# A two-layer decode attention step, forward and backward: score matmuls in column groups, one row layout for both layers, and a fixed TensorE order

## The chip, the cores and the metric

The kernel runs on one core of a Trainium2 chip. The metric is the device time of one execution in microseconds (us). Short names: TensorE is PE in the profile, VectorE is DVE, ScalarE is ACT, and SP (SPq for its queue) is the engine whose queue issues nearly all the loads.

## The reference

Two identical layers, each attention over a cache and then an MLP, and the gradients with respect to all inputs. One new token for each of 2 batches, 32 query heads on 4 key-value heads, 16384 cached keys, head size 128; all in bf16.

```python
x = x + attn(layernorm(x), k_cache, v_cache, wq, wo)   # layer 0
x = x + mlp(layernorm(x), w1, b1, w2, b2)              # layer 1
x = x + attn(layernorm(x), k_cache, v_cache, wq, wo)   # the same weights and cache again
x = x + mlp(layernorm(x), w1, b1, w2, b2)
out, vjp = jax.vjp(f, x, k_cache, v_cache, wq, wo, w1, b1, w2, b2)
return out, *vjp(grad_out)
```

The K and V caches are 33.5 MB each, and dK and dV have the same size. The attention that comes first in the network is called layer 1 here and the second one layer 3.

## The kernel before

The kernel goes over K and V four times: the two forward passes, the backward pass of layer 3 (dq alone, with P kept from the forward), and a last pass that does the backward of layer 1 and writes dK and dV for both layers. The first three are called "the three passes". Each has 8 chunks of 8.39 MB, and a chunk is four groups of 512 keys. K and V of a chunk come as 16 tiles of 512 KB (one for each of the 8 pairs of batch and kv head) into a ring of 24 buffers.

```python
def load_units(src4d, c, tag):                    # 8 loads of 512 KB
    units = []
    for g in range(NG):                           # NG = 8
        b, hk = divmod(g, HKV)
        u = AP_["ring"].tile([128, R, 128], BF, name="u_" + tag, tag="u")
        nc.sync.dma_start(u[:], src4d[b, hk, c * CH:(c + 1) * CH, :].rearrange("(p r) d -> p r d", r=R))
        units.append(u)
    return units

def xpose_group(units, r0, pool, tagname):        # 32 transposes, 4 evacuations (1 on ScalarE, 3 on VectorE)
    ...

def acc_matmuls(acc_ps, XT, units, l, r_list, r_off, first, last):   # O = P V, and dq = dS K
    for i, r in enumerate(r_list):
        for g in range(NG):
            j = 2 * l + g // 4                    # two of the four column groups for each layer
            nc.tensor.matmul(acc_ps[32 * j:32 * j + 32, (g % 4) * 128:(g % 4 + 1) * 128],
                             lhsT=XT[:, i, 32 * (g // 4):32 * (g // 4) + 32],
                             rhs=units[g][:, r_off + r, :], ..., tile_position=(0, 32 * j))

def attn_fwd_pass(l):
    rows = slice(64 * l, 64 * l + 64)             # each layer has its own 64 rows of P
    def XK(gi): ...                               # loads of a chunk, transposes of K
    def S(gi):                                    # scores, maximum, exponential
        sp = ps("mm").tile([128, 512], F32, name="sp", tag="mm")
        for g in range(NG):
            nc.tensor.matmul(sp[:], lhsT=qT_pad[l][:, g, :], rhs=d["kT"][:, g], start=(g == 0), stop=(g == NG - 1))
        ...                                       # reduce_max, min, Exp into P_sb, l_run
    def PT(gi): ...                               # 4 transposes of P, 1 evacuation
    def PV(gi): ...                               # O_g = acc_matmuls(...), O_sb = O_sb * beta + O_g
    XK(0); S(0)
    for gi in range(G):                           # G = 32 groups
        if gi + 1 < G: XK(gi + 1)
        if gi >= 1: PV(gi - 1)
        PT(gi)
        if gi + 1 < G: S(gi + 1)
    PV(G - 1)

def attn_bwd3_pass():                             # the same shape: XV, DP, DST, DQ
    ...
```

The order of calls in this loop is the order in which the program is written. A scheduler then decides the order on each engine, and in the kernel before it is free to do so on TensorE too. `qT_pad[l]` holds for each g a 128-column stationary matrix of which 8 columns are not zero, so that all 8 matmuls can add into one bank.

Of the kernel before, what the change touches and what calls it, by code (L numbers as in the profile page):

```python
# [36 lines left out]
def kernel(  # L37
# [35 lines left out]
    popen("wpool", 4)  # L73
    popen("wtp", 4)
    WP = dict(key="wpool", tag="w", shape=[128, WS])
# [202 lines left out]
    def proj_bwd(W, Din, Dout, dybf, name, cache=None):  # L278
# [9 lines left out]

        def gen():
            for view, j0, nj, n0, ncols in w_slabs(W, Din, Dout):  # L290
                for i in range(nj):
                    nblk = ncols // 128
                    for kb in range(0, nblk, 8):
                        yield (view, i, j0 + i, n0 // 128 + kb, kb, min(8, nblk - kb))

        def T(it):
            view, i, j, jn0, kb, nb = it
            tp = ps("tr").tile([128, 8, 128], BF, name="tp_w", tag="tr")
            for k in range(nb):
                nc.tensor.transpose(tp[:, k, :], view[:, i, (kb + k) * 128:(kb + k + 1) * 128], ident_bf[:])  # L300
            wT = P("wtp").tile([128, 8, 128], BF, name="wT", tag="wT")
            evac(wT[:, 0:nb], tp[:, 0:nb], "bf")
            return wT
# [106 lines left out]
    def build_pad(dst_pad, src_ps, l, mul=None):  # L410
        for g in range(NG):
            b, hk = divmod(g, HKV)
            o = dst_pad[:, g, 64 * l + 8 * g:64 * l + 8 * g + 8]
            i = src_ps[:, 8 * hk:8 * hk + 8, b]
            if mul is None:
                nc.vector.tensor_copy(o, i)
            else:
                nc.vector.tensor_scalar_mul(o, i, mul)  # L418
# [7 lines left out]
    def diag_to_loc(acc_sb, l, dstT, mul=None):  # L426
        for cb in range(4):
            tp = ps("sm").tile([128, 128], F32, name="tp_diag", tag="sm")
            nc.tensor.transpose(tp[:], acc_sb[:, cb * 128:(cb + 1) * 128], ident_f[:])
            for g in (cb, cb + 4):  # L430
                src = tp[:, 64 * l + 8 * g:64 * l + 8 * g + 8]
                if mul is None:
                    nc.vector.tensor_copy(dstT[:, 8 * g:8 * g + 8], src)
                else:
                    nc.vector.tensor_scalar_mul(dstT[:, 8 * g:8 * g + 8], src, mul)
# [23 lines left out]
    qT_pad = [ptile([128, NG, 128], BF, f"qT_pad{l}") for l in range(2)]  # L459
    for l in range(2):  # L460
        nc.gpsimd.memset(qT_pad[l][:], 0.0)
    dOT_pad = ptile([128, NG, 128], BF, "dOT_pad")
    nc.gpsimd.memset(dOT_pad[:], 0.0)
    O_sb = ptile([128, 512], F32, "O_sb")
    nc.gpsimd.memset(O_sb[:], 0.0)
    dq_sb = ptile([128, 512], F32, "dq_sb")
# [65 lines left out]
    def acc_matmuls(acc_ps, XT, units, l, r_list, r_off, first, last):  # L532
        n = len(r_list)
        for i, r in enumerate(r_list):
            for g in range(NG):
                j = 2 * l + g // 4
                nc.tensor.matmul(acc_ps[32 * j:32 * j + 32, (g % 4) * 128:(g % 4 + 1) * 128],  # L537
                                 lhsT=XT[:, i, 32 * (g // 4):32 * (g // 4) + 32],
                                 rhs=units[g][:, r_off + r, :],
                                 start=(first and i == 0 and g % 4 == 0), stop=(last and i == n - 1),  # L540
                                 skip_group_check=True, tile_position=(0, 32 * j))

    def attn_fwd_pass(l):
        rows = slice(64 * l, 64 * l + 64)
# [12 lines left out]
        def S(gi):  # L557
            d = stg_[gi]
            sp = ps("mm").tile([128, 512], F32, name="sp", tag="mm")
            for g in range(NG):  # L560
                nc.tensor.matmul(sp[:], lhsT=qT_pad[l][:, g, :], rhs=d["kT"][:, g], start=(g == 0), stop=(g == NG - 1))  # L561
# [22 lines left out]
        def PT(gi):  # L584
            tp = ps("tr").tile([128, 4, 64], BF, name="tp_p", tag="tr")
            for r4 in range(4):
                blk = gi * 4 + r4
                nc.tensor.transpose(tp[:, r4, :], P_sb[rows, blk * 128:(blk + 1) * 128], ident_bf[rows, rows])
            PTt = AP_["xTp"].tile([128, 4, 64], BF, name="PT", tag="PT")
# [3 lines left out]
        def PV(gi):  # L593
            c, rq = divmod(gi, 4)
            d = stg_.pop(gi)
            O_g = ps("o").tile([128, 512], F32, name="O_g", tag="o")
# [9 lines left out]
        XK(0)  # L606
        S(0)
        for gi in range(G):
            if gi + 1 < G:
                XK(gi + 1)  # L610
            if gi >= 1:
                PV(gi - 1)
            PT(gi)
            if gi + 1 < G:
                S(gi + 1)
# [10 lines left out]
    def p_fixup(l, kap):  # L626
        rows = slice(64 * l, 64 * l + 64)
# [4 lines left out]
    def attn_bwd3_pass():  # L632
        l = 1
        rows = slice(64, 128)
        G = NGRP
        dq_ps = ps("acc").tile([128, 512], F32, name="dq_ps", tag="acc")
# [11 lines left out]
        def DP(gi):  # L648
            d = stg_[gi]
            dp = ps("mm").tile([128, 512], F32, name="dp", tag="mm")  # L650
            for g in range(NG):
                nc.tensor.matmul(dp[:], lhsT=dOT_pad[:, g, :], rhs=d["vT"][:, g], start=(g == 0), stop=(g == NG - 1))  # L652
# [6 lines left out]
        def DST(gi):  # L659
            d = stg_[gi]  # L660
            tp = ps("tr").tile([128, 4, 64], BF, name="tp_ds", tag="tr")
            for r4 in range(4):
                nc.tensor.transpose(tp[:, r4, :], d["dS"][rows, r4 * 128:(r4 + 1) * 128], ident_bf[rows, rows])
            dST = AP_["xTp"].tile([128, 4, 64], BF, name="dST", tag="dST3", bufs=3)
# [11 lines left out]
        XV(0)  # L676
        DP(0)
        for gi in range(G):
            if gi + 1 < G:
                XV(gi + 1)  # L680
            DST(gi)
            if gi >= 1:
                DQ(gi - 1)
            if gi + 1 < G:
                DP(gi + 1)
# [7 lines left out]
    build_pad(qT_pad[0], q_ps, 0, mul=SCALE)  # L693
# [7 lines left out]
    WP_POOL = dict(key="wpool", tag="w", shape=[128, WS])  # L701
# [3 lines left out]
    def attn_out_and_mlp(l, x_inT, name, caches=None):  # L705
# [9 lines left out]
        p_fixup(l, kaps[l])  # L715
# [42 lines left out]
    build_pad(qT_pad[1], q_ps, 1, mul=SCALE)  # L758
# [41 lines left out]
    def attn_proj_bwd(l, gmid, name):  # L800
        nc.vector.tensor_copy(gaT_both[:, :, 2 * l:2 * l + 2], gmid[:])
        do_ps = proj_bwd(A_wo, DQ, D, gaT_both[:, :, 2 * l:2 * l + 2], "do" + name)
        build_pad(dOT_pad, do_ps, l)
        to_loc(doT_loc[l][:], do_ps[:])
        nc.vector.tensor_tensor(out=prodpad[:, 64 * l:64 * l + 64], in0=doT_loc[l][:], in1=oT_loc[l][:], op=ALU.mult)
# [28 lines left out]
    EV["cast"] = "SV"  # L834
    popen("wst", 16)
# [22 lines left out]
    qsum = tmp.tile([128, NG, 128], BF, name="qsum", tag="qsum")  # L858
    nc.vector.tensor_tensor(out=qsum[:], in0=qT_pad[0][:], in1=qT_pad[1][:], op=ALU.add)
    for src, dst in ((qsum, Q_bd), (dOT_pad, dO_bd)):  # L860
        tp = ps("tr").tile([128, NG, 128], BF, name="tp_bd", tag="tr")
        for g in range(NG):
            nc.tensor.transpose(tp[:, g, :], src[:, g, :], ident_bf[:])
# [18 lines left out]
    pclose("rowsp", "wst", "wtp", "wpool")  # L882
# [18 lines left out]
    dq_ps = ps("acc").tile([128, 512], F32, name="dq_ps4", tag="acc")  # L901
# [17 lines left out]
    def DP4(gi):  # L919
        d = st4[gi]  # L920
        dp = ps("mm").tile([128, 512], F32, name="dp4", tag="mm")
        for g in range(NG):
            nc.tensor.matmul(dp[:], lhsT=dOT_pad[:, g, :], rhs=d["vT"][:, g], start=(g == 0), stop=(g == NG - 1))
# [22 lines left out]
    def DST4(gi):  # L946
        d = st4[gi]
        tp = ps("tr").tile([128, 4, 64], BF, name="tp_ds4", tag="tr")
        for r4 in range(4):
            nc.tensor.transpose(tp[:, r4, :], d["dS"][0:64, r4 * 128:(r4 + 1) * 128], ident_bf[0:64, 0:64])  # L950
        dST = xT4.tile([128, 4, 64], BF, name="dST4", tag="dST")
# [43 lines left out]
    nc.vector.tensor_copy(dq_sb[0:64, :], dq_ps[0:64, :])  # L995
# [70 lines left out]
```

## Time and profile before

| | before |
|---|---|
| median of 16 runs | 1498.81 us (1489.9 to 1510.32) |
| profiled run | 1488.0 us |
| chunk to chunk, first forward pass | 24.3 us |
| chunk to chunk, second forward pass | 25.8 to 28.3 us |
| chunk to chunk, backward of layer 3 | 24.5 to 27.3 us |
| last pass, from its first load to the first weight load behind it | 403.0 us |

A chunk is read from the queue's timeline: the time from the first K load of one chunk to that of the next (in the forward passes from the third chunk on). Two lines of the page beside those shown in the prediction: the granted TensorE clock in 40 slices of the span (9 is 90% or more), and the chain of work that ended last.

```profile
PEclk9999996579999968899999889769899999999655
...
PE 47%; DMA 29%; DVE 11%; ACT 7%; issue 3%; SPq 1%; ACTq 0%; POOL 0%; DVEq 0%; another core or an unknown queue 0%
```

The clock falls towards half (digits 6, 5 and 7) where TensorE waits for weights, in slices 7 to 9, and is full in most slices of the passes. The chain names TensorE for 47% of the span and transfers for 29%. A chain tells what released each step, so a share of 47% says that TensorE set the pace more often than the transfers did.

### The profile page before, as it was taken

To read this page: it belongs to the slowest core of one execution; us is meant where nothing else is said; L and a number is where in the kernel's file an instruction comes from. 1 tells how busy PE (TensorE), PEld (TensorE's weight loads), DVE (VectorE), ACT (ScalarE), POOL (GpSimd) and SP (SyncE) were. 2 spreads that over 40 slices of the span, in tenths; PEclk is the share of its full clock that TensorE was granted. 3 is DMA by queue.
4 is the path that set the end of the run, shared out by engine and by line. 5 is a ranking of instruction groups with operands and counts; after the bars stand their busy time and mean duration, and the time that the engine had idled before them with its cause. 6 is when DMAs were issued, how large, how long until landed. Compare 5 with 4: busy or idle time off the path is not lost.

```text
span 1488.0 us, 38301 instructions
## 1 busy us (share of the span) xinstructions
PE 1203.0 (81%) x16349; PEld 818.1 (55%) x16500; DVE 807.2 (54%) x1649; ACT 487.2 (33%) x655; POOL 70.7 (5%) x132
## 2 busy tenths in 40 slices
PE   3899895578888779789888889989787878787576
PEld 3666664455555578766565767645343434443343
DVE  1666666146566764454444467655454545454465
ACT  0322220023223222311111245526444444544343
POOL 1000000000000000000000012110000000000243
PEclk9999996579999968899999889769899999999655
DMA  8998989998878972988897689769999999998985
GB/s 329 383 378 326 361 324 397 399 408 312 325 307 333 343 303 102 380 342 339 321 364 295 246 291 352 288 220 339 344 352 318 354 336 332 366 336 299 315 293 183
DMA packets 185023, 481.19 MB, mean 323 GB/s; under 512 B 20140, under 2 KB 20140, under 8 KB 184828
## 3 DMA queue, kind: packets, MB, share of 16 engines
q1 hardware_dynamic: 175156, 446.80, 81.8%
q0 software_dynamic: 9696, 31.93, 5.6%
q8 instruction: 129, 2.11, 0.6%
q14 instruction: 42, 0.34, 0.1%
HBM read 379.60 MB, written 98.58 MB: 321 GB/s over the span
## 4 chain that ended last, share of the span: by engine, by line
PE 47%; DMA 29%; DVE 11%; ACT 7%; issue 3%; SPq 1%; ACTq 0%; POOL 0%; DVEq 0%; another core or an unknown queue 0%
PE tp_x L525 12%; DMA u_vu<-in_A_v_cache_dram 7%; DMA u_ku<-in_A_k_cache_dram 7%; DMA out_dram<-stV 6%; PE tp_w L300 6%; PE sp L561 5%; DMA out_dram<-stK 4%; PE dp L652 4%; DMA wt<-in_A_wq_dram 4%; PE O_g L537 3%; PE dq_ps L537 3%; DVE xT_k L527 2%; PE dw_ps L393 2%; ACT xT_k L529 2%; PE tp_ip L275 2%
## 5 line engine op out<-in xcount | busy, mean ns | idle before, releaser
L527 DVE COPY xT_v<-tp_x 128x1024 bf16<-128x1024 bf16 x224 | 148.8, 688 | 121.7 <-PE tp_x L525 121.0
L525 PEld LDWEIGHTS <-u_vu 128*128 128x128 bf16 x2048 | 136.2, 100 | 65.3 <-issue 14.3
L525 PE MATMUL tp_x<-ident_bf,u_vu 128*128 128x128 bf16 x2048 | 165.4, 224 | 3.1 <-DMA u_vu<-in_A_v_cache_dram 1.5
L525 PE MATMUL tp_x<-ident_bf,u_ku 128*128 128x128 bf16 x2048 | 159.4, 225 | 6.3 <-DVE qT_pad L418 1.8
L527 DVE COPY xT_k<-tp_x 128x1024 bf16<-128x1024 bf16 x192 | 128.2, 686 | 54.1 <-PE tp_x L525 50.7
L525 PEld LDWEIGHTS <-u_ku 128*128 128x128 bf16 x2048 | 129.3, 100 | 49.2 <-DMA u_vu<-in_A_v_cache_dram 10.5
L561 PE MATMUL sp<-xT_k,qT_pad 128*128 128x512 bf16 x441 | 124.0, 387 | 37.9 <-DVE xT_k L527 23.7
L116 ACT CAST stK<-pk 128x1024 bf16<-128x1024 f32 x96 | 93.0, 1016 | 150.5 <-DMA out_dram<-stK 118.9
L300 PE MATMUL tp_w<-ident_bf,wt 128*128 128x128 bf16 x1472 | 132.3, 249 | 8.9 <-DMA wt<-in_A_wq_dram 7.4
L529 ACT COPY xT_k<-tp_x 128x1024 bf16<-128x1024 bf16 x64 | 64.8, 1012 | 216.3 <-PE tp_x L525 216.2
L114 DVE COPY wT<-tp_w 128x1024 bf16<-128x1024 bf16 (+1 forms) x124 | 81.3, 678 | 70.2 <-PE tp_w L300 61.9
L963 PE MATMUL pk<-Q_bd,dS_g 128*128 128x512 bf16 x240 | 81.4, 403 | 42.7 <-ACT stK L116 34.5
L300 PEld LDWEIGHTS <-wt 128*128 128x128 bf16 x1472 | 103.5, 112 | 22.3 <-issue 13.3
L116 ACT CAST stV<-pv 128x1024 bf16<-128x1024 f32 x96 | 95.3, 1013 | 58.0 <-PE pv L943 34.1
L537 PE MATMUL O_g<-u_vu,PT 128*32 128x128 bf16 x2048 | 99.4, 221 | 2.4 <-DVE PT L114 1.0
L943 PE MATMUL pv<-dO_bd,P_sb 128*128 128x512 bf16 x225 | 85.8, 455 | 18.9 <-ACT stV L116 8.3
L116 ACT COPY wT<-tp_w 128x1024 bf16<-128x1024 bf16 (+1 forms) x64 | 63.5, 992 | 99.3 <-PE tp_w L300 88.5
L537 PE MATMUL dq_ps<-u_ku,dST 128*32 128x128 bf16 x2048 | 80.6, 221 | 11.0 <-DVE dST L114 9.0
L114 DVE CAST dwst<-dw_ps 128x512 bf16<-128x512 f32 (+1 forms) x88 | 76.5, 879 | 22.8 <-PE dw_ps L393 22.5
L116 ACT CAST dwst<-dw_ps 128x512 bf16<-128x512 f32 (+1 forms) x88 | 64.9, 742 | 72.8 <-PE dw_ps L393 68.6
L537 PEld LDWEIGHTS <-PT 128*32 128x32 bf16 x2048 | 67.4, 96 | 36.3 <-issue 18.9
L529 ACT COPY xT_v<-tp_x 128x1024 bf16<-128x1024 bf16 x32 | 32.4, 1012 | 165.7 <-PE tp_x L525 161.9
(245 smaller groups left out, 1421.5 us busy)
## 6 DMA issues: line engine op xcount, KB each, us to landing
u_ku<-in_A_k_cache_dram SPq DMA_DIRECT2D x192, 512.0 KB, 8.3
u_vu<-in_A_v_cache_dram SPq DMA_DIRECT2D x192, 512.0 KB, 9.8
wt<-in_A_wo_dram SPq DMA_DIRECT2D x64, 512.0 KB, 8.8
u_vu<-in_A_v_cache_dram SPq DMA_DIRECT2D x128, 256.0 KB, 5.3
u_ku<-in_A_k_cache_dram SPq DMA_DIRECT2D x128, 256.0 KB, 6.4
out_dram<-stV SPq DMA_DIRECT2D x128, 256.0 KB, 6.3
out_dram<-stK SPq DMA_DIRECT2D x128, 256.0 KB, 6.3
wt<-in_A_wq_dram SPq DMA_DIRECT2D x48, 512.0 KB, 9.5
```

Source lines behind the costliest of these rows:

```text
L114: nc.vector.tensor_copy(out, in_)
L116: nc.scalar.copy(out, in_)
L275: nc.tensor.transpose(tp[:, k, :], cache[:, j, (kb + k) * 128:(kb + k + 1) * 128], ident_bf[:])
L300: nc.tensor.transpose(tp[:, k, :], view[:, i, (kb + k) * 128:(kb + k + 1) * 128], ident_bf[:])
L525: nc.tensor.transpose(tp[:, g2, r4, :], units[2 * gh + g2][:, r0 + r4, :], ident_bf[:])
L527: nc.vector.tensor_copy(xT[:, 2 * gh:2 * gh + 2], tp[:])
L529: nc.scalar.copy(xT[:, 2 * gh:2 * gh + 2], tp[:])
L537: nc.tensor.matmul(acc_ps[32 * j:32 * j + 32, (g % 4) * 128:(g % 4 + 1) * 128], lhsT=XT[:, i, 32 * (g // 4):32 * (g // 4) + 32], rhs=units ...
L561: nc.tensor.matmul(sp[:], lhsT=qT_pad[l][:, g, :], rhs=d["kT"][:, g], start=(g == 0), stop=(g == NG - 1))
L652: nc.tensor.matmul(dp[:], lhsT=dOT_pad[:, g, :], rhs=d["vT"][:, g], start=(g == 0), stop=(g == NG - 1))
L943: nc.tensor.matmul(pv[:, half * 512:(half + 1) * 512], lhsT=P_sb[:, colb:colb + 128], rhs=dO_bd[:, half * 512:(half + 1) * 512], start=Tru ...
L963: nc.tensor.matmul(pk[:, half * 512:(half + 1) * 512], lhsT=d["dS"][:, r4 * 128:(r4 + 1) * 128], rhs=Q_bd[:, half * 512:(half + 1) * 512], ...
```

## The change

The intent is to take matmul work off TensorE in the three passes and to keep the scheduler from breaking up its sequence there. Its core, with the repeated edits of the other passes left out:

```diff
+    def ct_matmuls(out_ps, stat_ct, xT):          # scores and dp, in all passes
+        for b in range(2):
+            for hk in range(HKV):
+                g = 4 * b + hk
+                nc.tensor.matmul(out_ps[32 * hk:32 * hk + 32, :], lhsT=stat_ct[:, g, :], rhs=xT[:, g],
+                                 start=(b == 0), stop=(b == 1), tile_position=(0, 32 * hk))
...
-            for g in range(NG):
-                nc.tensor.matmul(sp[:], lhsT=qT_pad[l][:, g, :], rhs=d["kT"][:, g], start=(g == 0), stop=(g == NG - 1))
+            ct_matmuls(sp, qT_ct, d["kT"])
...
-    qT_pad = [ptile([128, NG, 128], BF, f"qT_pad{l}") for l in range(2)]
+    qT_ct = ptile([128, NG, 32], BF, "qT_ct")     # columns 16*l + 8*b .. +8 of group hk
-    O_sb = ptile([128, 512], F32, "O_sb")
+    O_sb = ptile([128, 256], F32, "O_sb")
...
     def acc_matmuls(...):
-            for g in range(NG):
-                j = 2 * l + g // 4
-                nc.tensor.matmul(acc_ps[32 * j:32 * j + 32, (g % 4) * 128:(g % 4 + 1) * 128],
-                                 lhsT=XT[:, i, 32 * (g // 4):32 * (g // 4) + 32], ..., tile_position=(0, 32 * j))
+            for b in range(2):
+                for hk in range(HKV):
+                    nc.tensor.matmul(acc_ps[32 * hk:32 * hk + 32, b * 128:(b + 1) * 128],
+                                     lhsT=XT[:, i, 32 * hk:32 * hk + 32], ..., tile_position=(0, 32 * hk))
...
-        rows = slice(64 * l, 64 * l + 64)
+        rows = slice(0, 128)
...
-        XK(0)
-        S(0)
-        for gi in range(G):
-            ...
+        with tc.manual_schedule(engines={mybir.EngineType.PE}):     # TensorE in program order
+            XK(0)
+            S(0)
+            for gi in range(G):
+                ...
...
-        p_fixup(l, kaps[l])
+        if l == 1:
+            p_fixup(l, kaps[l])
...
-    popen("wpool", 4)                             # first projection: 4 weight buffers
-    WP = dict(key="wpool", tag="w", shape=[128, WS])
+    WP = dict(key="ring", tag="u", shape=[128, R, 128])              # the ring of 24
```

A column group is 32 of the 128 columns of the stationary side; `tile_position=(0, 32 * hk)` chooses one of the four. The two layers can share 128 rows of P because row 32 x hk + 16 x l + 8 x b now belongs to kv head hk, layer l and batch b, and each layer's other rows are harmless. The rest of the diff follows from this layout or changes nothing in the instruction stream.

## The prediction

> **What bounds the kernel now.** I read the page first, then a table of stages (busy time of each engine, granted clock and DMA share in chosen stretches), then the queue's own waits, then the TensorE timeline of one chunk.
>
> The page's busy line and its DMA slices:
>
> ```profile
> PE 1203.0 (81%) x16349; PEld 818.1 (55%) x16500; DVE 807.2 (54%) x1649; ACT 487.2 (33%) x655; POOL 70.7 (5%) x132
> ...
> DMA  8998989998878972988897689769999999998985
> GB/s 329 383 378 326 361 324 397 399 408 312 325 307 333 343 303 102 380 342 339 321 364 295 246 291 352 288 220 339 344 352 318 354 336 332 366 336 299 315 293 183
> ```
>
> TensorE and DMA are both busy most of the time, and the mix changes by stage. So the question is which of the two ends last in each stage. The table by stage (one chunk is 8.39 MB of K and V, four groups of 512 keys):
>
> ```profile
> core 0: us, PE busy (x) PEld busy (x) DVE busy (x) ACT busy (x) POOL busy (x), PEclk, DMA share, GB/s
> ...
> 35.26:66.97 31.71, 28.19 (x330) 19.44 (x336) 17.17 (x36) 10.45 (x18) 0.00 (x0) 1.00 1.03 410
> ...
> 91.31:115.65 24.34, 22.01 (x301) 15.22 (x307) 15.92 (x37) 7.21 (x16) 0.00 (x0) 1.00 0.91 358
> ...
> 418.50:444.00 25.50, 21.73 (x299) 14.90 (x304) 16.47 (x37) 7.72 (x16) 0.00 (x0) 1.00 0.84 331
> ...
> 718.36:743.06 24.70, 21.62 (x304) 14.85 (x305) 11.96 (x20) 4.05 (x4) 0.00 (x0) 1.00 0.89 342
> ...
> 817.20:831.00 13.80, 12.80 (x218) 9.23 (x217) 7.53 (x13) 2.02 (x2) 0.00 (x0) 1.00 0.01 2
> ...
> 1010.00:1386.00 376.00, 299.26 (x2789) 161.49 (x2831) 182.35 (x254) 181.73 (x186) 1.54 (x3) 0.93 1.00 337
> ```
>
> In the three passes over K and V (first forward 35 to 232, second forward 311 to 522, backward of layer 3 from 640 to 831) TensorE is busy 22 of 24.3 to 25.8 us, while DMA has gaps: the same loads ran at 410 GB/s when the first buffers filled. In the last backward pass (1010 to 1386) it is the other way round, DMA share 1.00. The row 817 to 831 shows a tail without any DMA, which each pass has in some form.
>
> One chunk of the first pass, microsecond by microsecond, and the queue's own waits over five chunks:
>
> ```profile
> 92.00:93.00 1.00, 0.95 (x19) 0.62 (x19) 0.87 (x2) 0.00 (x0) 0.00 (x0) 1.00 0.21 82
> 93.00:94.00 1.00, 1.00 (x23) 0.66 (x19) 1.00 (x4) 0.00 (x0) 0.00 (x0) 1.00 0.08 33
> ...
> 103.00:104.00 1.00, 0.86 (x15) 0.64 (x16) 0.87 (x3) 0.20 (x3) 0.00 (x0) 1.00 1.04 422
> ```
>
> ```profile
> SPq L513 <- PE O_g L537: 44.7, 6, 9.9
> SPq L513 <- PE tp_x L525: 23.5, 31, 3.3
> SPq L513 <- DMA u_ku<-in_A_k_cache_dram: 16.1, 21, 0.9
> ```
>
> DMA runs at 400 to 420 GB/s, then stops for some 3 us per chunk, because the queue waits for ring buffers that TensorE has not released (O_g: the last reads of V; tp_x: the last reads of K). The passes are TensorE bound, with DMA only 15% below its own limit.
>
> **The Trainium skill.** "TensorE: Matmul & The Clock Gate", Part 3, says that matmuls with few stationary columns can be put side by side in column groups of 32, and gives 2.38 times for three such tiles of 512 columns. The trace has no such score matmul, but its O_g matmuls use two column groups and go at 31 ns where a full-array one of the same 128 columns takes 60 ns (below), so it agrees for two. "TensorEngine Tiling (Array Packing)", Key Properties, says that a change of tiling mode drains the array; the trace agrees: a lone O_g matmul between score matmuls takes 0.16 us from start to start, not 0.03. "DMA: Bandwidth & Descriptors", Specifications, has a fabric ceiling of 435 GB/s; the trace held 410 over 32 us. The clock page's Part 1 says that an idle window halves the TensorE clock; the trace agrees, 0.54 and 0.50 in the two stretches from 232 to 311 where TensorE waits for weights.
>
> **The change, part by part.**
>
> TensorE timeline of before, one chunk:
>
> ```profile
> 95.66 1.50 PE L525 MATMUL tp_x<-ident_bf,u_ku 128*128 128x128 bf16 x24
> 97.09 0.23 PE L537 MATMUL O_g<-u_vu,PT 128*32 128x128 bf16 x1
> ...
> 99.20 0.23 PE L537 MATMUL O_g<-u_vu,PT 128*32 128x128 bf16 x1
> 99.36 1.25 PE L561 MATMUL sp<-xT_k,qT_pad 128*128 128x512 bf16 x5
> 100.45 0.39 PE L525 MATMUL tp_x<-ident_bf,u_ku 128*128 128x128 bf16 x4
> ...
> 104.76 1.62 PE L537 MATMUL O_g<-u_vu,PT 128*32 128x128 bf16 x50
> 106.32 1.04 PE L561 MATMUL sp<-xT_k,qT_pad 128*128 128x512 bf16 x3
> ```
>
> Start to start: a transpose (95.66 to 97.09)/24 = 60 ns, a score matmul (99.36 to 100.45)/5 = 218 ns, an O_g matmul 1.56/50 = 31 ns.
>
> 1. Scores and dp. Before, each of the 8 head groups ran a 128-column stationary that held 8 useful columns, all adding into one bank: 8 x 218 = 1.74 us per group of keys. After, four kv heads sit in four column groups and two batches add up: two rounds instead of eight, 2 x 218 = 0.44 us. Saved 1.3 us per group; over 128 groups 167 us of TensorE, of which 32 groups are in the DMA-bound last pass.
> 2. Fixed TensorE order in the three passes. Before, the scheduler cut the groups of matmuls to pieces, the lone O_g above is one. Per group 32 x 0.060 + 1.74 + 4 x 0.055 + 32 x 0.031 = 4.87 us, 19.5 per chunk, but busy is 22.0; the other 2.5 us are switches. After, four switches a group at about 0.13 us, so 32 x 0.060 + 0.44 + 0.22 + 1.0 + 0.5 = 4.1 us per group, 16.4 per chunk.
> 3. O_g and dq go over four column groups instead of two, still 32 matmuls and 32 weight loads. I count no gain.
> 4. Layer 1 and 3 share 128 rows of P. O_sb update 128x256 instead of 64x512: 0.74 to about 0.46 us. The PT evacuation doubles, 0.28 to about 0.42. VectorE per group: 3 x 0.69 + 0.68 + 0.30 + 0.21 + 0.46 + 0.42 = 4.1 us. The exponential has the same length, 0.68.
> 5. The first fix-up of P is gone: 32 multiplications of 0.3 us, but they ended at 242.8 and the next VectorE work began at 247.6, so only about 1.5 us between 232 and 238 lay on the path.
> 6. The first projection uses the 24-buffer ring in place of four buffers: the queue issues 16 weight slabs and 8 K tiles without the wait of before (third to sixteenth slab trickled until 27). (33 us x 405 GB/s - 11.4 MB moved by 35)/405 = about 4 us.
> 7. Small additions: prodpad in 8 pieces twice (about 1 us each), the embedded copies for Q_bd and dO_bd about 3 us of VectorE before the last pass, two transposes fewer at each diagonal (1 us). Near zero in sum.
>
> What ends last afterwards: with TensorE at 4.1 and VectorE at 4.1 us and their handovers about 4.2 to 4.5 us a group, a chunk costs 17 to 18 us of compute and 8.39 MB / 0.41 = 20.5 us of DMA. The three passes become DMA bound. From the start to the second pass's output projection the kernel moves 107 MB (weights and first pass) + 67.1 + 8.4 = 182.6 MB; at 402 GB/s, the mean of the saturated stretches, 454 us, + 3 at the start and 3 for the end, 460 against 528: 68 us. Backward of layer 3: 75.5 MB / 0.405 = 186 from 597, then a tail of about 11 us, 794 against 830: 36 us. Together 104 us if DMA never stops. I don't believe that fully: compute (18 us, plus about 1.7 us waiting for V, plus one half-clock window of 1 to 2 us per chunk) comes close to 20.5, and I take 21.5 us a chunk. 24 chunks x 1.0 = 24 us lost. The last pass stays DMA bound; I take 3 us of gain for the shorter fills. Sum 104 - 24 + 3 + 0 = 83, and 1494 - 83 = 1411, rounded to 1412.
>
> **The rivals.**
> (a) TensorE now waits for data and its clock falls. For: 0.50 where it waited for weights, 0.88 in the chunk from 364 to 393. Against: waits of some 3 us per chunk, spread out, and 1.00 with 90% busy. If the clock fell to 0.75 in the passes, a group would take 5.2 us and a chunk about 22.7: 24 x 2.2 = 53 lost instead of 24, so 1441.
> (b) The fixed order exposes the chain score, maximum, exponential, transpose. The order of after puts the next transposes and the previous O_g between, about 3 us, against 0.7 + 0.2 + 1.0 (an evacuation ahead on ScalarE) + 0.7 + 0.2 = 2.8: just hidden. If not, 5.5 us a group, 22 a chunk, 1424.
> (c) DMA never stops: 1388.
> (d) The last pass also gains, as its staging buffers or ring free earlier. For: its rate varies between 290 and 406 GB/s. Against, its queue's waits, nearly all for transfers of its own:
>
> ```profile
> SPq L977 <- DMA u_ku<-in_A_k_cache_dram: 42.3, 106, 1.1
> SPq L897 <- DMA u_vu<-in_A_v_cache_dram: 35.0, 96, 1.6
> ...
> SPq L977 <- DVE stV L114: 9.8, 2, 7.2
> SPq L897 <- PE pv L943: 8.5, 29, 0.6
> ```
>
> Waits on engines sum to about 29 of 376 us; if half of it went, 15 us, so 1397.
> (e) The column-group matmuls don't overlap (weights not loaded ahead): 8 x 218 stays, and only the switches are saved, 2 us a chunk: about 1445.
>
> **Range and chances.** Rivals (a), (b) and (e) give the upper side, (c) with (d) the lower. 8 in 10 between 1378 and 1448. Below 1464 is faster by over 2%: 0.94; within 2%: 0.05; slower: 0.01, for a stall that none of these names.
>
> **What would show it.** Chunks of both forward passes and of the layer-3 backward at 20.5 to 22 us, 380 GB/s and more, DMA share near 1.0, TensorE busy near 16; score matmuls in runs of 8 within about 0.5 us; the queue's waits on O_g mostly gone; the last pass still about 376 us. Wrong would be: chunks of 24 us with DMA gaps (b or e), a granted clock under 0.9 in the passes (a), or a last pass over 10 us shorter (d).

## The result, and the profile after

| | before | after |
|---|---|---|
| median | 1498.81 us, 16 runs | 1389.86 us, 11 runs (1383.85 to 1391.85) |
| profiled run | 1488.0 us | 1387.3 us |
| ratio | 1 | 0.9263 (0.9237 to 0.9288) |

A ratio is the mean time of one kernel's runs over that of the other's runs in the same rounds, with a 95% interval, so it is not quite the ratio of the medians. Executions over 1.5% slower than the fastest of the same kernel are left out of the means. The change is faster by 7.4%, and the time lies 22 us under the point of the prediction, inside its range.

The page of after: TensorE's busy time, its clock, the DMA share in slices, and the chain.

```profile
PE 1044.3 (75%) x16444; PEld 714.2 (51%) x16492; DVE 789.8 (57%) x1648; ACT 481.3 (35%) x655; POOL 68.1 (5%) x131
...
PEclk9989895579898597888989898799889898989555
DMA  8999999999999956999988897699999999998974
...
DMA 64%; PE 21%; DVE 5%; ACT 4%; SPq 3%; issue 2%; POOL 0%; DVEq 0%; ACTq 0%; another core or an unknown queue 0%; POOLq 0%
```

TensorE is busy 159 us less than before (1203.0). The DMA row now has a 9 in nearly every slice of the three passes, where before it went between 7 and 9. The clock is granted a little less often. The chain has turned over: transfers 64% and TensorE 21%, against 29% and 47%.

The table of stages of after, for one chunk of each of the three passes and for most of the last pass. The columns are the stretch and its length, then busy time and instruction count of PE, PEld, DVE, ACT and POOL, then granted clock, DMA share and GB/s.

```profile
90.97:111.54 20.57, 16.21 (x312) 11.95 (x315) 15.69 (x37) 7.13 (x16) 0.00 (x0) 0.92 1.02 404
317.77:337.91 20.14, 15.62 (x283) 11.13 (x287) 15.37 (x36) 7.13 (x16) 0.00 (x0) 0.92 1.02 408
683.47:704.00 20.53, 15.08 (x308) 11.46 (x307) 12.23 (x20) 4.05 (x4) 0.00 (x0) 0.92 1.03 408
...
910.00:1287.00 377.00, 282.00 (x2776) 137.26 (x2818) 186.79 (x254) 179.26 (x184) 1.54 (x3) 0.89 1.01 337
```

A chunk takes 20.1 to 20.6 us here in all three passes, the DMA share is over 1.0 at 404 to 408 GB/s, and TensorE is busy 15 to 16 us. The last row, the last pass, is as it was: 337 GB/s and a DMA share of 1.01.

One group of the first pass on TensorE, after. The first column is the start, the second the length; the time between two starts is what an entry costs.

```profile
132.99 0.61 PE L552 MATMUL sp<-xT_k,qT_ct 128*32 128x512 bf16 x8
133.54 1.51 PE L529 MATMUL tp_x<-ident_bf,u_ku 128*128 128x128 bf16 x24
...
135.85 0.63 PE L542 MATMUL O_g<-u_vu,PT 128*32 128x128 bf16 x32
136.41 0.40 PE L599 MATMUL tp_p<-ident_bf,P_sb 128*128 128x128 bf16 x4
136.74 0.61 PE L552 MATMUL sp<-xT_k,qT_ct 128*32 128x512 bf16 x8
```

The 8 score matmuls take 0.55 us from start to start (132.99 to 133.54) and are in one piece. The 32 O_g matmuls take 0.56 us (135.85 to 136.41), 17.5 ns each. From one score run to the next is 3.75 us (132.99 to 136.74), so a chunk would need 15.0 us of TensorE if it never waited.

What it does wait for, between 90 and 195 us, about five chunks: the queue's waits, then TensorE's.

```profile
SPq L517 <- DMA u_ku<-in_A_k_cache_dram: 31.4, 38, 1.1
SPq L517 <- PE O_g L542: 20.1, 6, 5.1
```

```profile
PE tp_x L529 <- DMA u_ku<-in_A_k_cache_dram: 13.6, 17, 1.1
PE O_g L542 <- DMA u_vu<-in_A_v_cache_dram: 5.2, 7, 1.1
```

TensorE now waits for K and V themselves, 18.8 us in five chunks or 3.8 us a chunk, which is not among its waits in before's first pass. The queue's largest wait is for its own earlier transfers. Its wait on O_g has fallen from 44.7 us to 20.1 us but has not gone, and yet the DMA share stays over 1.0: with 24 buffers in the ring, the queue can stand at a buffer that isn't free while earlier loads still fill the engines. A wait of the queue is a loss only where the DMA row shows a gap with it.

Where the time came from, read from the queue's timeline (us):

| stretch | before | after | saved | predicted |
|---|---|---|---|---|
| start to the end of the second pass's output projection | 528.25 | 465.79 | 62.5 | 68 |
| from there to the first weight load of the backward | 66.5 | 66.3 | 0.2 | 0 |
| that load to the end of layer 3's backward | 235.5 | 200.1 | 35.4 | 36 |
| middle stage | 156.7 | 154.0 | 2.7 | 0 |
| last pass | 403.0 | 400.5 | 2.5 | 3 |
| rest | 98.0 | 100.5 | -2.5 | 0 |

The sum is 100.8 us; the spans differ by 100.7. The column "predicted" stands before the 24 us of lost DMA time that the prediction took off the three passes.

### The profile page after: what moved, and what is told of

Its sections match the earlier page's. It is cut to its first block, busy times and chain, and to the rows that moved or that the text cites. A ratio compares the mean times of both kernels' runs of the same rounds, so it can differ in the third digit from the quotient of the medians.

```text
span 1387.3 us, 38345 instructions
## 1 busy us (share of the span) xinstructions
PE 1044.3 (75%) x16444; PEld 714.2 (51%) x16492; DVE 789.8 (57%) x1648; ACT 481.3 (35%) x655; POOL 68.1 (5%) x131
## 4 chain that ended last, share of the span: by engine, by line
DMA 64%; PE 21%; DVE 5%; ACT 4%; SPq 3%; issue 2%; POOL 0%; DVEq 0%; ACTq 0%; another core or an unknown queue 0%; POOLq 0%
DMA u_ku<-in_A_k_cache_dram 24%; DMA u_vu<-in_A_v_cache_dram 20%; PE tp_w L301 6%; DMA out_dram<-stK 6%; DMA out_dram<-stV 5%; DMA wt<-in_A_wq_dram 4%; DMA wt<-in_A_wo_dram 3%; PE dw_ps L396 2%; PE tp_ip L274 2%; PE tp_x L529 2%; DMA wt<-in_B_w_dram 2%; DVE wT L113 1%; PE pb_dn L312 1%; SPq L1000 1%; PE pv L962 1%
## 5 line engine op out<-in xcount | busy, mean ns | idle before, releaser
L529 PE MATMUL tp_x<-ident_bf,u_ku 128*128 128x128 bf16 x2048 | 163.8, 238 | 62.9 <-DMA u_ku<-in_A_k_cache_dram 51.2
L529 PE MATMUL tp_x<-ident_bf,u_vu 128*128 128x128 bf16 x2048 | 168.4, 229 | 38.9 <-DMA u_vu<-in_A_v_cache_dram 33.6
L529 PEld LDWEIGHTS <-u_ku 128*128 128x128 bf16 x2048 | 134.1, 107 | 107.7 <-DMA u_ku<-in_A_k_cache_dram 66.9
L301 PEld LDWEIGHTS <-wt 128*128 128x128 bf16 x1472 | 103.5, 112 | 21.3 <-issue 17.3
L962 PE MATMUL pv<-dO_bd,P_sb 128*128 128x512 bf16 x226 | 88.7, 466 | 22.7 <-ACT stV L115 11.6
L113 DVE CAST dwst<-dw_ps 128x512 bf16<-128x512 f32 (+1 forms) x88 | 76.4, 879 | 21.3 <-PE dw_ps L396 21.1
L113 DVE CAST stK<-pk 128x1024 bf16<-128x1024 f32 x32 | 39.1, 1221 | 79.6 <-DMA out_dram<-stK 36.8
L552 PE MATMUL dp<-xT_v,dOT_ct 128*32 128x512 bf16 x512 | 74.6, 415 | 2.0 <-DVE xT_v L531 1.8
L312 PEld LDWEIGHTS <-wT 128*128 128x128 bf16 x1472 | 55.3, 100 | 36.5 <-DVE wT L113 20.1
L261 PEld LDWEIGHTS <-wt 128*128 128x128 bf16 x1472 | 44.0, 105 | 50.4 <-issue 19.9
```

The source lines that it names most:

```text
L113: nc.vector.tensor_copy(out, in_)
L261: nc.tensor.matmul(pt[:, jn, :], lhsT=view[:, i, k * 128:(k + 1) * 128], rhs=xbf[:, j, :], start=first, stop=(j == Jin - 1), skip_group_ch ...
L301: nc.tensor.transpose(tp[:, k, :], view[:, i, (kb + k) * 128:(kb + k + 1) * 128], ident_bf[:])
L312: nc.tensor.matmul(pt[:, j, :], lhsT=wT[:, k, :], rhs=dybf[:, jn, :], start=(jn == 0), stop=(jn == Jout - 1))
L529: nc.tensor.transpose(tp[:, g2, r4, :], units[2 * gh + g2][:, r0 + r4, :], ident_bf[:])
L552: nc.tensor.matmul(out_ps[32 * hk:32 * hk + 32, :], lhsT=stat_ct[:, g, :], rhs=xT[:, g], start=(b == 0), stop=(b == 1), tile_position=(0, ...
```

## The experiments

Two questions were open. First, what made the passes of before slow: the amount of matmul work, or the order in which the scheduler had put it? Second, do the transfers really bound the passes of after, so that the parts of the change overlap in what they are worth? Theory 1 is the prediction's: TensorE's work bounds the passes of before, transfers those of after, and order and column groups each take away a share of TensorE's work. The rivals, such as one part alone doing everything, or transfers bounding the kernel before as well, stand in each expectation.

The mean time of a chunk (from the third to the eighth first K load of a forward pass, from the second to the eighth of the backward, us) of all kernels in one table; each is told below.

| kernel | forward, layer 1 | forward, layer 3 | backward, layer 3 | time, us | ratio |
|---|---|---|---|---|---|
| before | 24.3 | 26.3 | 25.1 | 1498.81 | 1 |
| after | 20.8 | 20.6 | 20.7 | 1389.86 | 0.9263 |
| order_only | 21.5 | 21.1 | 21.2 | 1410.81 | 0.9382 |
| no_order | 24.1 | 23.5 | 20.9 | 1428.22 | 0.9501 |
| padded | 20.7 | 21.3 | 20.8 | 1393.74 | 0.9263 |
| padded_no_order | 23.8 | 23.8 | 23.0 | 1451.97 | 0.9674 |
| order_alternate | 21.2 | 21.1 | 21.2 | 1412.43 | 0.9381 |
| small_undone | 20.8 | 21.1 | 20.9 | 1396.77 | 0.9280 |
| prefetch | 20.7 | 21.1 | 20.4 | 1382.90 | 0.9192 |
| half_before | 21.1 | 21.1 | 21.1 | 1399.32 | one run |
| half_order_only | 21.1 | 21.1 | 21.1 | 1397.30 | one run |
| half_pinned_before | 24.4 | 25.7 | 26.5 | 1501.10 | one run |
| half_no_order | 15.4 | 15.3 | 14.9 | 1252.28 | one run |
| half_after | 15.1 | 15.2 | 15.0 | 1259.07 | one run |

The first eight rows below "before" gave correct results. The halved kernels give a wrong result.

### order_only: the fixed order alone

```diff
 # before, in both pass functions
+        with tc.manual_schedule(engines={mybir.EngineType.PE}):
             XK(0)
             ...
```

> The kernel before with nothing changed but the fixed TensorE order in the three passes; score and dp matmuls stay 8 full-array ones. Theory 1 (both parts shorten TensorE work, and each pass then runs into the 20.5 us of DMA a chunk): TensorE needs 4.87 us plus four switches of 0.13, 5.4 us a group, 21.5 us a chunk, so chunks of 21.5 to 22.5 us against 24.3 to 25.8, and 1495 - 24 x 2.7 = about 1430. Rival 2 (the column groups do it all, the order is incidental): chunks stay at 24 us or more, 1485 to 1500.

Measured: 1410.81 us (1410.27 to 1413.46), ratio 0.9382 (0.9351 to 0.9413), against a before of 1504.52 in the same rounds. The stage table and TensorE's timeline of order_only:

```profile
90.26:111.36 21.10, 20.05 (x310) 14.75 (x304) 15.75 (x37) 7.11 (x16) 0.00 (x0) 1.00 1.01 398
```

```profile
115.70 1.08 PE L537 MATMUL O_g<-u_vu,PT 128*32 128x128 bf16 x32
...
116.93 1.90 PE L561 MATMUL sp<-xT_k,qT_pad 128*128 128x512 bf16 x8
```

This one edit, which removes no instruction, gives 6.2 of the 7.4%. TensorE is busy 20.05 us a chunk instead of 22.0, and its idle time falls from 2.3 to 1.05 us. The score matmuls are still the padded ones, 1.74 us for eight (116.93 to 118.67, where the next transposes start). The rival of a small gain has fallen, and so has the size that theory 1 gave: I had expected about 1430.

### no_order: everything but the fixed order

```diff
 # after, in both pass functions
-        with tc.manual_schedule(engines={mybir.EngineType.PE}):
```

> The changed kernel without the fixed order; column groups, layout and the rest stay. Theory 1: TensorE saves 8 x 218 - 0.54 = 1.2 us a group, 4.8 us a chunk of the 22 us busy, so about 17 us busy, under the 20.5 us of DMA: chunks of 20.7 to 21.5, 1390 to 1410. Rival 3 (the fixed order does it all, as switches between tiling modes eat what the column groups save): 1430 to 1470.

Measured: 1428.22 us (1426.38 to 1434.17), ratio 0.9501 (0.9464 to 0.9538). Theory 1 was wrong here: I had expected 1390 to 1410, with the column groups enough by themselves. Two neighbouring chunks in the stage table of no_order:

```profile
94.21:118.84 24.63, 19.90 (x315) 13.87 (x304) 15.15 (x37) 7.43 (x16) 0.00 (x0) 0.86 0.89 343
118.84:141.10 22.26, 17.47 (x314) 11.94 (x304) 14.96 (x37) 7.43 (x16) 0.00 (x0) 1.00 0.97 366
```

Chunks of about 25 and 22.3 us alternate in the forward passes, with a clock of 0.86 in the slow one shown and a DMA share of 0.89. The slow one has 2.4 us more of TensorE busy time (19.90 against 17.47) for nearly the same instructions and is 2.4 us longer, so what sets the two apart goes with the clock; the rest of the excess over after's 20.8 us is in both. In this stretch TensorE waits for VectorE's and ScalarE's evacuations of K (12.6 us in 106 us) and of P (3.6 us) and for the exponential (2.7 us), and never for a transfer. The backward pass, where there is no maximum and no exponential between the scores and their use, runs at 20.9 us a chunk, as in after. This fits a free order that is costly where a chain across engines lies between two pieces of TensorE work, but it is read from the waits: the passes also differ in the order that the scheduler gave them. What the run does show is that less matmul work alone does not bring the forward chunks down to the transfers.

### padded: the fixed order with the old score matmuls

```diff
 # after: the 32-column stationaries embedded in 128 columns
-        ct_matmuls
+        for g in range(NG):
+            nc.tensor.matmul(out_ps[:], lhsT=em[:, g, :], rhs=xT[:, g], start=(g == 0), stop=(g == NG - 1))
```

> The changed kernel with the fixed order, but scores and dp by 8 full-array matmuls on a stationary embedded in 128 columns (results unchanged). Theory 1: the group takes 3.75 us as measured in the changed kernel plus 8 x 218 - 540 = 1.2 us, 4.95 us, 19.8 us a chunk, and some waiting for V: at the limit, 20.7 to 22 us a chunk, 1390 to 1420. Rival 2: chunks back at 24 us, 1470 or more.

Measured: 1393.74 us (1391.05 to 1395.38), ratio 0.9263 (0.9231 to 0.9295): the same ratio as the full change. One chunk:

```profile
127.80:148.24 20.44, 18.60 (x309) 13.24 (x306) 15.10 (x37) 7.14 (x16) 0.00 (x0) 1.00 1.03 408
```

TensorE is busy 18.6 us rather than 16.2 and gets the full clock, and the chunk is as long as in after, because the transfers end last either way. The part that the prediction put first, the column groups for the scores, is worth nothing that these runs resolve (the intervals are 0.3% to either side) once the rest is there.

### padded_no_order: neither

The two edits above together.

> The changed kernel with both main parts undone: full-array score matmuls and the scheduler's order; the shared 128 rows, four column groups for O_g and dq, the ring for the first projection and the dropped fix-up stay. Theory 1: TensorE about 22 us a chunk again less some 1.7 us as O_g goes at 17.5 instead of 31 ns: chunks of 22.5 to 24, 1440 to 1480. If the rest of the change (O_g, ring, fix-up) were what counts: under 1420.

Measured: 1451.97 us (1447.21 to 1462.59), ratio 0.9674 (0.9616 to 0.9733), 23.8 us a chunk forward and 23.0 backward with TensorE busy 20.8 us and a DMA share of 0.92. What is left here is the shared rows, the four column groups for O_g and dq, and the small parts, in the scheduler's order. With order_only this gives a table of two by two for the structure of after:

| | scheduler's order | fixed order |
|---|---|---|
| padded scores | 0.9674 | 0.9263 |
| scores in column groups | 0.9501 | 0.9263 |

The column groups are worth 1.8% in the scheduler's order and nothing in the fixed one. The 1.8% is not theirs alone, since the scheduler wrote a different order for each of the two kernels of that column. The parts do not add up, and it has no meaning to ask what share "is" the column groups'.

### half_after, half_order_only, half_before and half_no_order: half the bytes

To see what compute alone costs, each K and V tile is loaded to half, and its second half reads the first again. All instructions of the three passes but the size of their loads stay; their order, as it turned out, does not always. Done for after, order_only, before and no_order, one run each, where the kernel before took 1492.76.

```diff
-            nc.sync.dma_start(u[:], src...)
+            nc.sync.dma_start(u[:, 0:HR, :], src...[:, 0:HR, :])        # HR = R // 2
-                ... units[...][:, r0 + r4, :]
+                ... units[...][:, r0 % HR + r4, :]
```

> Wrong result on purpose: the changed kernel, but the three passes load only the first half of every K and V tile and use it twice, so the instructions on all engines are the same and DMA in the passes halves (8.39 to 4.19 MB a chunk). Theory 1 (the changed passes are bound by DMA, with compute to spare): chunks fall from 20.6 us to the compute floor, 4 x 3.75 = 15 us, so some 24 x 5.5 = 130 us less, about 1260. Rival (the passes sit at a compute or latency limit that happens to equal 20.6): nothing changes.

> Wrong result on purpose: halved loads in the kernel before with the fixed order only. Its chunks took 21.1 us at 20.05 us of TensorE busy. Theory 1: TensorE sets them, 5.27 us a group, so they stay at 21.1 and the time falls by less than 15 us, 1395 to 1410. Rival: DMA set them already and they fall below 20.

> Wrong result on purpose: the same halved loads in the kernel before. Theory 1 (its passes are bound by TensorE work and its order, DMA only follows): the chunks stay at 23.5 to 25 us, and the time falls only by the faster first fill, 1470 to 1495. Rival (the 3 us gaps of DMA and the waits on ring buffers, a cycle of transfer and release, set the period): chunks fall well under 22 us, 1430 or less.

> Wrong result on purpose: halved loads in the changed kernel without the fixed order. Its forward chunks took 22.3 and 25.5 us in turn, its backward ones 20. If the scheduler's order, with the waits between engines that it exposes, sets the forward chunks, they stay at 22 or more and only the backward ones fall, to about 17: 1400 or so. If it is the cycle of ring release and transfer, the forward chunks fall to 17 to 19 as well, 1300 or so.

Measured: 1259.07, 1397.3, 1399.32 and 1252.28 us. One chunk of half_after and one of half_order_only:

```profile
68.67:83.67 15.00, 14.02 (x309) 10.92 (x306) 14.66 (x37) 7.14 (x16) 0.00 (x0) 1.00 0.87 287
```

```profile
86.90:108.00 21.10, 20.05 (x310) 14.75 (x304) 15.74 (x37) 7.09 (x16) 0.00 (x0) 1.00 0.60 202
```

With half the bytes after's chunk falls from 20.6 to 15.0 us, and its VectorE is then busy 14.66 of 15.00 us and its TensorE 14.02. So the transfers bound the passes of after, with over 5 us a chunk to spare. The chunk of order_only stays at 21.10 us to the hundredth, at a DMA share of 0.60: it is TensorE bound, although with full loads it shows a share of 1.01 (its row above). A DMA share near 1 does not prove that transfers are the bound; two engines can sit at the same figure.

half_before missed theory 1 by far (I had expected 1470 to 1495), with 21.1 us a chunk, the rival's number. But the comparison was not clean. The scheduler had written another TensorE order for it: short loads changed where it put things. Counted in the built kernels over the three passes, the sequence falls into 974 runs of like matmuls in before, 576 in half_before, and 383 in order_only. half_before's is regular, the same for each group of a pass, with one O_g matmul, or a run of four, set apart, and half_no_order's nearly so (595 runs against 966 in no_order). half_no_order's 1252.28 us lies below both figures of its expectation, 1400 and 1300, and says as little of no_order's own order. So half_before and half_no_order tell what a regular order costs, and not what before's order costs.

### half_pinned_before: half the bytes in before's own order

TensorE's instructions of the three passes were put, one by one, into the order that before has, as recorded from the built kernel, and held there by the same fixed-order block. TensorE's sequence is then equal to before's; the orders of VectorE and ScalarE differ in places.

```diff
+ORDER = ["K20S2K4S4K39S2K1S7P4S1K24O1K8O2S1O1P4S6...", ...]   # before's sequence, K transposes, S scores, ...
+        with tc.manual_schedule(engines={mybir.EngineType.PE}):
+            replay(ORDER[l], K=..., S=..., P=..., O=...)
```

> Wrong result on purpose: halved loads in the kernel before, with the TensorE order of the kernel before pinned instruction by instruction in the three passes (the earlier run with halved loads turned out to have got a different order from the scheduler: 24 transposes, 1 O_g, 8 transposes, 31 O_g, 4 P transposes, 8 scores, in every group). Theory 1a (the order by itself costs the time, by switches and by waits on VectorE and ScalarE): chunks stay at 24 to 25.5 us though DMA is out of the way, about 1485. Rival 1b (the order is harmless and the ring's cycle of release and transfer cost the time): chunks at 21.1 as in the earlier run, about 1400.

Measured: 1501.1 us, against a before of 1506.04. One chunk:

```profile
92.07:116.46 24.39, 22.54 (x310) 15.25 (x304) 16.10 (x38) 7.20 (x16) 0.00 (x0) 1.00 0.56 174
```

With half the bytes to move and before's order the chunk is 24.39 us, as before's 24.34 (the later passes have 25.7 and 26.5, against 26.3 and 25.1). So the order itself, and not the transfers, put before's chunk some 3 us above the 21.1 us that the same matmuls take in order_only. It also shows that the fixed-order block gains nothing by itself: with a bad order held in it the kernel stays slow. The time is 16 us over the 1485 of theory 1a. TensorE is busy 22.5 us, and it waits 7.9 us in five chunks for VectorE's copies of K, ahead of the scores, the same figure as in before in the same stretch.

### order_alternate: does alternating two column groups do what four do?

The O_g matmuls cost 32 ns in order_only and 17.5 ns in after. Before takes four of one column group in a row, after goes through the groups in turn. This run takes before's two groups in turn.

```diff
 # order_only
-            for g in range(NG):
+            for g in (0, 4, 1, 5, 2, 6, 3, 7):
```

> The kernel before with the fixed order, and in O_g and dq the two column groups alternate (g 0, 4, 1, 5 ...) in place of four matmuls in one group and then four in the other. In the changed kernel an O_g matmul takes 17.5 ns, here 32 before this edit. If alternating is what counts: 17.5 to 20 ns, chunks at 20.5 us, 0.6 us x 24 = 14 us under the fixed order alone, about 1397. If four column groups are needed: stays at 27 to 32 ns and about 1410.

Measured: 1412.43 us (1408.05 to 1416.73), ratio 0.9381 (0.9348 to 0.9414), as order_only. TensorE's timeline:

```profile
116.57 1.07 PE L537 MATMUL O_g<-u_vu,PT 128*32 128x128 bf16 x32
117.57 0.29 PE L588 MATMUL tp_p<-ident_bf,P_sb 64*128 64x64 bf16 x4
```

32 matmuls still take 1.00 us (116.57 to 117.57), 31 ns each. So the turn alone does nothing, and the gain comes with four groups, which before could not have: each layer owned only two. The single records of the traces agree: between 90 and 195 us the starts of O_g matmuls come in pairs about 56 ns apart in order_only and order_alternate alike, and in fours about 55 ns apart in after.

### small_undone: the first projection and the first fix-up put back

```diff
 # after
+    popen("wpool", 4)
+    WP = dict(key="wpool", tag="w", shape=[128, WS])
-        if l == 1:
-            p_fixup(l, kaps[l])
+        p_fixup(l, kaps[l])
```

> The changed kernel with two small parts undone: the first projection through its pool of four buffers, and the fix-up of P after the first pass back (it has no effect on the result, as the second pass overwrites P). Theory: K loads start about 8 us later, the first pass ends 4 to 9 us later; the fix-up costs under 2 us, hidden now behind the output projection's weights: 1393 to 1401. Rival: nothing, as later DMA gaps absorb it.

Measured: 1396.77 us (1392.15 to 1400.94), ratio 0.9280 (0.9253 to 0.9306) against after's 0.9263 (0.9237 to 0.9288). The intervals overlap, so the runs don't settle it. In the traces the first output weight is loaded at 192.58 us instead of 190.60, and the second pass starts at 269.45 instead of 266.48: 2 to 3 us, where the prediction had 4 and 1.5, and the expectation an end of the first pass 4 to 9 us later.

### prefetch: filling the gaps that after has left

After has stretches without any transfer, such as the 7 us at the end of the third pass (725.20 to 732.20, DMA share 0.01). Four more weight buffers let the first four slabs of the next weights come while the pass ends; four V tiles of the third pass's last chunk use them too, to free ring buffers.

```diff
 # after
+    popen("wpre", 4)
     def wtile(name):
+        if PRE[0] > 0:
+            PRE[0] -= 1
+            t = P("wpre").tile([128, R, 128], BF, name=name, tag="wp")
+            return t[:].rearrange("p r d -> p (r d)")
...
+        if l == 1:
+            PRE[0] = 4            # also before the two backward projections
```

> The changed kernel with a pool of four buffers, which the old weight pool freed, used to fill DMA gaps: some slabs of the output projection's weights before the layer-3 backward pass and four slabs of A_wq are loaded while DMA is idle. If DMA bytes in the saturated stretches set the time: 2 to 3 slabs at 1.3 us before the pass and up to 5 us at its end, 3 to 8 us less than the changed kernel, 1382 to 1387. Rival: the stage after the pass is bound by TensorE and absorbs it: no change within 2 us.

Measured: 1382.9 us (1380.41 to 1388.99), ratio 0.9192 (0.9167 to 0.9216), so 0.8% below after by the two ratios, which are from different rounds and whose intervals do not overlap. The first K load of the third pass starts at 554.88 us instead of 559.51, the next weights are loaded from 720.67 instead of 732.19, while the pass still runs (its last matmuls end at 726.2 instead of 732.2), and the first K load of the last pass stands at 880.42 instead of 890.11. It gives 4 us back at the start, where the scheduler put four weight slabs ahead of the first pass (its first K load is at 23.50 us instead of 19.45). In a kernel bound by transfers, an idle queue is the place to look.

## Why the prediction was right or wrong

**What bounds the kernel: right for the bound, incomplete for the reason.** TensorE set the pace in the passes of before. The prediction read this as too much work, 22 us in 24.3. The pinned run shows that the order made the difference between 24.3 us and the 21.1 us that the same work needs, and order_only shows what it cost: 2.0 us of busy time a chunk and 1.3 us of waits. The prediction had the first part among its 2.5 us of switches. It had no entry for the second part, the waits that a free order puts between engines.

**Step 1, the score matmuls: right as work, wrong as the main gain.** 8 of them went from 1.74 to 0.55 us; the prediction had 0.44 without a switch. In time it is worth nothing beside the other parts, as padded shows, because the chunk had already fallen to what the transfers need. By the prediction's terms it was needed: 17 to 18 us of compute and the 4 x 1.3 = 5.2 us that it saves are 22 to 23, over the 20.5 of the transfers. By the measured ones it was not: 15.0 + 4 x (1.74 - 0.55) = 19.8.

**Step 2, the fixed order: right in kind, and much larger.** The prediction left four switches a group at 0.13 us, which is 2.0 us a chunk, so by its own numbers the order alone saved 0.5 of the 2.5 us of switches. (Rival (e) puts that saving at 2 us a chunk; the two don't fit.) The order alone saved 3.2 us in the chunks shown (24.34 to 21.10). A switch in a regular order costs less than 0.13 us. A group of order_only is 5.27 us from O_g to O_g (115.70 to 120.97), against 4.87 us of work in the prediction plus 0.26 us of a wait on ScalarE's copy, which leaves about 0.14 us for all switches of a group where the prediction had 0.5.

**Step 3, O_g and dq over four column groups: wrong.** "I count no gain", and it is 17.5 ns instead of 31 or 32, 0.44 us a group and 1.8 us a chunk. This step and the one before make up the error of TensorE's group: predicted 4.1 us, and 3.5 of busy time in half_after (14.02 / 4), 3.75 from start to start; 0.1 us each that the scores and the larger transposes of P took beyond their terms went the other way. The gain of padded over order_only, 1.3% by the ratios, is this step and the small parts together; no run took it alone.

**Step 4, VectorE: each term right, the sum too high.** The O_sb update took 0.475 us and the copy of P 0.42, as predicted. But the sum of 4.1 us a group counts each record in full, and VectorE's busy time was 14.66 / 4 = 3.67. Neighbouring records overlap: two copies with 0.68 us each have together 1.28.

**Steps 5 to 7: small.** 2 to 3 us in the trace for 5 and 6 against 5.5 (the sum shown for step 6 comes to 4.9 us, not 4); the time does not resolve it, and no run took 7 alone.

**The sum: the term that was mis-sized is the 24 us of lost DMA time.** The prediction had 104 us if the transfers never stop, and took 24 us off, as it thought that 18 us of compute with its waits would come too close to 20.5 us of transfers. Compute is 15.0 us, so chunks took 20.6 to 20.8 us instead of the 21.5 that I took. Of the 104 us, 97.9 came (62.5 + 35.4). Rival (c), 1388 us, is what happened, and the last pass brought 2.5 us where 3 had been predicted. That the total came near is owed to the transfers, which bound the passes whatever the parts of TensorE's work are worth: step 1 brought no time of its own, steps 2 and 3 brought more than they were given, and the total does not show it. The base of 1494 us also lies 5 us under the median of 1498.81; as gains, 83 us stand against 109.

**Rival (a) happened and did not matter.** The clock did fall: the prediction's own sign for it, under 0.9 in the passes, is there in about half of the chunks (0.83 or 0.84), and the others have 0.91 or more. Two rows of a table in steps of 1 us, of after:

```profile
99.00:100.00 1.00, 0.17 (x3) 0.17 (x4) 0.69 (x1) 0.00 (x0) 0.00 (x0) 1.00 1.01 401
...
103.00:104.00 1.00, 1.00 (x14) 0.60 (x7) 0.60 (x2) 0.00 (x0) 0.00 (x0) 0.50 1.05 418
```

TensorE works 0.17 us in the first, waiting for K, and a little later runs at half clock, from about 102.6 to 106. The prediction gave "one half-clock window of 1 to 2 us per chunk" and that is its size here, 3.4 us at half speed or 1.7 us of work. Other chunks lose twice as much:

```profile
153.62:174.21 20.59, 17.68 (x321) 12.61 (x324) 15.36 (x36) 7.13 (x16) 0.00 (x0) 0.83 1.02 403
```

But with 5 us of room a chunk it is paid from the waiting: this chunk, at 0.83, takes 20.59 us, and the one at 0.92 above 20.57. (The rival's 5.2 us a group at a clock of 0.75 is 5.5 by its own terms, 4.1 / 0.75.) half_after, with more pressing work, has a clock of 1.00.

**Rivals (b) and (e) did not happen:** a group needs 3.75 us, not 5.5, and the score matmuls overlap. (d) did not happen either.

What stays open: why the scheduler's order for no_order costs what it does in the forward passes is read from its waits and its clock and was not tested with that order pinned. How much of the 1.3% between order_only and padded is O_g and how much the shorter VectorE work was not tried.

## What to carry to other kernels

Before counting matmuls to remove, look at the timeline for lone instructions between runs of another kind: a free order can cost more than the matmuls that a rewrite would remove, and holding it may bring most of the gain (6.2 of 7.4% here). Once a stage reaches the bound of its transfers, further savings there are worth nothing in time, so compute each stage's floor on every engine and test it, for example by halving the bytes. When an experiment changes a transfer or a size, check that the order on the engines is still the same before comparing times.

## What the Trainium skill lacked or had wrong

- "TensorE: Matmul & The Clock Gate", Part 1, has a floor of about 25 ns from start to start however small the matmul. In four column groups 32 matmuls of 128 moving columns, each with weights of its own, took 0.56 us, 17.5 ns each. In two groups they took 31 to 32 ns, whether the two alternate or not. Its Part 3 has about 4 ns between the starts of tiles that run side by side, from matmuls of 512 columns, and no figure for 128.
- The same Part 1 lets the clock fall after an idle window of about 3.4 us; it also says that short idle gaps between groups of matmuls made it go up and down in one kernel, without saying how short or how many. Here no single wait of TensorE between 90 and 195 us was longer than 1.1 us, and the clock still fell to 0.50 for about 3.4 us, soon after a stretch of 4 us (97 to 101) in which TensorE was busy for about a third of the time.
- "TensorEngine Tiling (Array Packing)", Key Properties, says that a change of mode drains the array and gives no figure. A lone matmul among others took 0.16 us instead of 0.03, but in a regular order all switches of a group together cost about 0.14 us; the 22.0 us of TensorE in a chunk fell to 20.05 with the order alone.
- "DMA: Bandwidth & Descriptors", Specifications, gives ceilings of 435 and about 358 GB/s, and its table of measurements 425 GB/s for 16 MB loaded while the neighbouring core is idle. Loads alone ran at 404 to 408 GB/s here over whole chunks, so the 358 did not bind this one core. The last pass, which reads and writes, ran at 337 GB/s with a DMA share of 1.01, and the page has no figure for such a mix.
- No page says that the scheduler's order on one engine depends on the size of the transfers. Halving the loads alone changed before's TensorE sequence in the three passes from 974 to 576 runs of like matmuls and its chunk from 24.3 to 21.1 us, while the pinned sequence stayed at 24.4.
